# One pool of nine weight tiles, loaded in the order of use, in a fused attention and gated feed-forward kernel

## The chip, the cores and the metric

The kernel runs on one core of a Trainium2 chip. The metric is the time of one execution in microseconds (us), and the median of several runs where there are several. The profiled execution comes with its own time and with its span, from the first to the last instruction that the profile records.

## What is computed

For 2048 tokens of width 1024 (bf16), after a layer norm without scale and bias:

```python
xn = layernorm(x)
q, k, v = split(xn @ wqkv)                  # 32 heads of 32
# each token looks at itself and 7 earlier tokens, 2 apart
logits = einsum(q, k[pos - 2*w]) * 32**-0.5 # w = 0..7, masked below position 0
o = softmax(logits) weighted sum of v[pos - 2*w]
s = o @ wo
g = silu((silu(xn @ w1) * (xn @ w3)) @ w2)  # 3584 hidden columns
out = x + s * g
```

Here w1 and w3 are 1024 x 3584, w2 is 3584 x 1024, wqkv is 1024 x 3072, wo is 1024 x 1024.

## The kernel before

**Tiling.** The tokens are worked on in four blocks of 512 (`c` = 0 to 3). All matrix products are on TensorE (PE), as matmuls of a 128x128 weight tile by 512 columns, accumulated over the contraction. For each block the order on PE is: the qkv projection (`qkv`, line 289; 192 matmuls), the up projections by w1 and w3 (`up_block`, line 270; 14 column blocks `fb` of 32 matmuls each), the first half of the down projection by w2 (`down_half` with `dh` = 0, line 463; 7 tiles of 16 matmuls), the second half (`dh` = 1, again 7 tiles), with the output projection by wo (`wo_proj`, line 432; 64 matmuls) put into it. In block 0 three up blocks come ahead of the qkv projection (`LEAD`), and wqkv is first loaded raw, reordered on VectorE (DVE) and ScalarE (ACT), used from the reordered tiles `pm`, and written to a scratch tensor `wperm`, from which later blocks load it. In block 3 `wo_proj` stands between the two halves, and the second half is `last_half` (line 498), token tile by token tile.

**The attention.** Logits, softmax and the weighted sum run on DVE and ACT beside the matmuls. They are cut into small items in `Side`, which deals them out between the matmuls by costs written by hand. Two shuffles across partitions go through DMAs that GpSimd (POOL) issues: `L` from `E` (line 349) and `Pr` from `pb` (line 390). The weighted sum `oT` (lines 401 and 412) has to be complete before `wo_proj` of the block.

**The weights.** No weight but wo and the raw wqkv is held: each block streams the others again, in tiles of 512 KB (4 KB on each of 128 partitions). All of these loads are issued on the queue of SyncE (SP), which issues in the order of the program and stands still while the instruction at its head waits. A load waits for the last matmul that read the tile whose place it takes. There are two pools:

- `wstream`, six tiles: w1, w3 and the q tiles (from `wperm`). `load_w()` (line 167) issues the next of `w_list`, `take_w` hands out the oldest. At the end of the list stand four w2 tiles for `last_half`.
- `w2s`, three tiles: w2. `load_w2()` (line 185) and `take_w2` do the same with `w2_list`.

An up block loads two further tiles when its own two are used up, but not in its last three column blocks (`AHEAD` = 3). A qkv tile loads one. In the down projection each used w2 tile loads the w2 tile three further on, and `late_w` loads q tiles for the next block (in block 3: the four w2 tiles) at positions written out by hand: in block 0 at tiles 6, 7, 8, 9, 11 and 12 of 14, in blocks 1 and 2 at 1, 3, 5, 7, 9 and 11. Three w2 tiles are loaded before the loop over the blocks, ahead of their use by the whole up projection.

**What shares the SP queue.** Also on SP: the input tiles `x_t` of the next block (line 214), their transposes into `xnT_next` (line 238), `wo` (line 196, eight DMAs of 256 KB), the residual `xres` (line 488, 1 MB), and the writes to `wperm` (line 686). In block 0, `wo` is loaded after down tiles 0 and 2 and `xres` after tile 4; in the other blocks `wo` after up blocks 11 and 12 and `xres` after up block 13. Every load of every queue runs on the same 16 DMA engines of the core.

Of the kernel before, what the change touches and what calls it, by code (L numbers as in the profile page):

```python
# [9 lines left out]
BF16 = mybir.dt.bfloat16  # L10
# [35 lines left out]
def kernel(  # L46
# [11 lines left out]
    nc = tc.nc  # L58
    P = 128
# [4 lines left out]
    NCH = S // CH  # L64
    NST = CH // P
    FT = F // P
    FB = FT // 2
# [4 lines left out]
    LEAD = 3  # L72
    WO_AT = 3
    WO_AT0 = 6
    AHEAD = 3
    PV_GATE = (13.0, 20.0, 20.0, 18.0)
    scale = float(Dh) ** -0.5

# [4 lines left out]
    w2_r = B_w2.rearrange("(ft p) n -> p ft n", p=P)  # L83
# [7 lines left out]
    xp = ctx.enter_context(tc.tile_pool(name="x", bufs=NST))  # L91
    small = ctx.enter_context(tc.tile_pool(name="small", bufs=4))
    xnT_pool = ctx.enter_context(tc.tile_pool(name="xnT", bufs=2))
    wstream = ctx.enter_context(tc.tile_pool(name="wstream", bufs=6))
    w2s = ctx.enter_context(tc.tile_pool(name="w2s", bufs=3))
    qkv_pool = ctx.enter_context(tc.tile_pool(name="qkv", bufs=1))
    hp = ctx.enter_context(tc.tile_pool(name="hT", bufs=FT))
    sgp = ctx.enter_context(tc.tile_pool(name="sg", bufs=3))
# [13 lines left out]
    for st in range(2):  # L112
# [12 lines left out]
        out=ident[:], in_=ident[:], compare_op=ALU.not_equal, fill=1.0,  # L125
# [5 lines left out]
        out=maskb[:], in_=maskb[:], compare_op=ALU.is_ge, fill=-1.0e9,  # L131
# [7 lines left out]


    w_list = []
    for fb in range(LEAD):
        w_list += [("1", fb), ("3", fb)]
    for fb in range(LEAD, FB):
        w_list += [("1", fb), ("3", fb)]
    for c in range(1, NCH):
        w_list += [("q", b) for b in range(12)]
        for fb in range(FB):
            w_list += [("1", fb), ("3", fb)]
    w_list += [("2", fb) for fb in range(4)]  # L150
    w_next = iter(w_list)
    w_tiles = deque()

    def load_w():
        item = next(w_next, None)
        if item is None:
            return
        kind, i = item
        wt = wstream.tile([P, KT, 2 * P], BF16, tag="w")
        if kind == "q":  # L160
            src, dst = wperm[:, :, 2 * i:2 * i + 2, :].rearrange("kt kp tj p -> kp kt (tj p)"), wt[:]
        elif kind == "2":
            src = w2_r[:, i * 4:(i + 1) * 4, 512:1024]
            dst = wt[:].rearrange("p a b -> p (a b)").rearrange("p (i n) -> p i n", n=512)
        else:
            src, dst = (w1_r if kind == "1" else w3_r)[:, :, i * 256:(i + 1) * 256], wt[:]
        nc.sync.dma_start(out=dst, in_=src)  # L167
        w_tiles.append((item, wt if kind != "2" else dst))

    def take_w(item):  # L170
        got, wt = w_tiles.popleft()
        assert got == item, (got, item)
        return wt

    w2_list = [(c, dh, fb) for c in range(NCH) for dh in range(2) for fb in range(7) if (c, dh) != (NCH - 1, 1) or fb >= 4]
    w2_next = iter(w2_list)
    w2_tiles = deque()

    def load_w2():
        item = next(w2_next, None)  # L180
        if item is None:
            return
        c, dh, fb = item
        wt = w2s.tile([P, 4, 512], BF16, tag="w2")
        nc.sync.dma_start(out=wt[:], in_=w2_r[:, fb * 4:(fb + 1) * 4, dh * 512:(dh + 1) * 512])
        w2_tiles.append((item, wt))

    def take_w2(item):
        got, wt = w2_tiles.popleft()
        assert got == item, (got, item)  # L190
        return wt

# [58 lines left out]
    def bring_one():  # L251
        if brings and brings[0][0] <= side.now:
            brings.popleft()[1]()

    def gate_up(g_ps, u_ps):
        sg = sgp.tile([P, CH], BF16, tag="sg")
        nc.scalar.activation(out=sg[:], in_=g_ps[:], func=ACTF.Silu)  # L257
        ht = hp.tile([P, CH], BF16, tag="ht")
        nc.vector.tensor_mul(ht[:], sg[:], u_ps[:])  # L259
        return ht  # L260

    def up_block(c, xnT, fb):
        hts = []
        w1t, w3t = take_w(("1", fb)), take_w(("3", fb))
        for i in range(2):
            pss = []
            for wt in (w1t, w3t):
                ps = psum_mm.tile([P, CH], FP32, tag="mm", name=f"gu{c}_{fb}_{len(pss)}")
                for kt in range(KT):
                    nc.tensor.matmul(  # L270
                        ps[:], lhsT=wt[:, kt, i * P:(i + 1) * P], rhs=xnT[:, kt, :],
                        start=(kt == 0), stop=(kt == KT - 1),
                    )
                pss.append(ps)
            if i == 1 and fb < FB - AHEAD:
                load_w()
                load_w()
            hts.append(gate_up(*pss))
            if c == 0 or c == NCH - 1 or fb < FB - 1:
                side.step(2 * GRP, 0.7)  # L280
            else:
                side.now += 2 * GRP
            bring_one()
        return hts
# [156 lines left out]
    def silu_acc(acc, w=512):  # L441
        gt = ep.tile([P, 512], FP32, tag="gt", bufs=5)
        nc.scalar.activation(out=gt[:, 0:w], in_=acc, func=ACTF.Silu)  # L443
        return gt

    def finish(c, st, c0, w, gt, s_sb, xres, queue):
        g0 = (c * NST + st) * P
        o_t = ep.tile([P, 512], BF16, tag="o_t")
        nc.vector.tensor_mul(gt[:, 0:w], gt[:, 0:w], s_sb[:, st, c0:c0 + w])  # L449
        nc.vector.tensor_add(o_t[:, 0:w], gt[:, 0:w], xres[:, st, c0:c0 + w])  # L450
        queue.dma_start(out=out_flat[g0:g0 + P, c0:c0 + w], in_=o_t[:, 0:w])  # L451

    def down_half(c, dh, hts, at=None):
        accs = [psum_mm.tile([P, 512], FP32, tag="mm", name=f"acc{c}_{dh}_{st}") for st in range(NST)]
        gts = []
        for fb in range(7):
            w2t = take_w2((c, dh, fb))
            order = [(i, st) for i in range(4) for st in range(NST)]
            if fb in (0, 6):
                order = [(i, st) for st in range(NST) for i in range(4)]  # L460
            for n, (i, st) in enumerate(order):
                f = fb * 4 + i
                nc.tensor.matmul(  # L463
                    accs[st][:], lhsT=hts[f][:, st * P:(st + 1) * P], rhs=w2t[:, i, :],
                    start=(f == 0), stop=(f == FT - 1),
                )
                if n == 7:
                    side.step(GRP)
            load_w2()
            late_w(c, dh, fb)  # L470
            if fb == 6:
                gts = [silu_acc(accs[st][:]) for st in range(NST)]
            side.step(GRP)
            if at is not None:
                at(fb)
        return gts

    def late_w(c, dh, fb):
        at = dh * 7 + fb
        if c + 1 < NCH:  # L480
            if at in ((6, 7, 8, 9, 11, 12) if c == 0 else (1, 3, 5, 7, 9, 11)):
                load_w()
        elif at in (1, 3, 5, 6):
            load_w()

    def load_xres(c):
        xres = block("xres").rearrange("p (st d) -> p st d", st=NST)
# [2 lines left out]

    def last_half(c, hts, s_sb, xres):
        dh = 1
        w2ts = [take_w(("2", fb)) for fb in range(4)] + [take_w2((c, dh, fb)) for fb in range(4, 7)]
        for st in range(NST):
            for c0, cut in ((0, 384), (384, 128)) if st == NST - 1 else ((0, 512),):
                acc = psum_mm.tile([P, 512], FP32, tag="mm", name=f"acc{c}_{dh}_{st}_{c0}")
                for f in range(FT):
                    nc.tensor.matmul(  # L498
                        acc[:, 0:cut], lhsT=hts[f][:, st * P:(st + 1) * P],
                        rhs=w2ts[f // 4][:, f % 4, c0:c0 + cut],  # L500
                        start=(f == 0), stop=(f == FT - 1),
                    )
                gt = silu_acc(acc[:, 0:cut], cut)
                finish(c, st, dh * 512 + c0, cut, gt, s_sb, xres, nc.sync)
# [71 lines left out]
    def part0(k, st):  # L576
# [24 lines left out]
        out=junk[:], in_=x0[2][:], func=ACTF.Square, bias=nm[:], scale=1.0 / 32.0, accum_out=mv0[2][:, 1:2],  # L601
# [74 lines left out]
    for t in range(3):  # L676
# [8 lines left out]
        for half in range(2):  # L685
            nc.sync.dma_start(
                out=wperm[half * 4:(half + 1) * 4, :, t * NJ:(t + 1) * NJ, :].rearrange("kt kp j p -> kp kt (j p)"),
                in_=pmh[t, half].rearrange("kp kt j p -> kp kt (j p)"),
            )
    for _ in range(3):  # L690
        load_w2()


    for c in range(NCH):
# [3 lines left out]
        for fb in range(LEAD if c == 0 else 0, FB):  # L698
            blk_hts = up_block(c, xnT, fb)
            hts = hts + blk_hts if hts is not None else blk_hts  # L700
            if c > 0 and fb in (11, 12):
                was.append(load_wo(fb - 11))
            if c > 0 and fb == 13:
                res["x"] = load_xres(c)
        while brings:
            brings.popleft()[1]()
        def early(fb, c=c, res=res, was=was):
            if c == 0 and fb == 4:
                res["x"] = load_xres(c)
            if c == 0 and fb in (0, 2):  # L710
                was.append(load_wo(fb // 2))

        gts = down_half(c, 0, hts, early)
        xres = res["x"]
        if c + 1 < NCH:
# [51 lines left out]
```

## Time and profile before

| | |
|---|---|
| time, median of 3 runs | 818.49 us (818.47 to 820.02) |
| profiled execution: time / span | 818.31 us / 816.5 us |
| mean granted clock of TensorE | 0.999 of full |
| DVE / ACT / POOL busy | 481.7 us (59%) / 205.8 us (25%) / 92.3 us (11%) |
| moved by DMA | 152.69 MB, mean 187 GB/s |
| weight tiles from w1, w3, w2 | 168 loads of 512 KB, median 4.5 us from issue to landing |
| q tiles from `wperm` | 36 loads of 512 KB, median 4.5 us |

Lines such as L463 are lines of the kernel. "A <- B" after an operation names what it writes and reads; in a list of waits it names who waited for whom. The chain of waits is followed back from the last instruction: each piece is the work that the next piece had to wait for, so the pieces add up to the span. In tables by stretch of time, "DMA share" is the mean busy share of the 16 DMA engines; it can read slightly above 1.

### The profile page before, as it was taken

The numbers are of one execution on the slowest core, as the hardware profiler recorded it, in microseconds if no ns is written. First come the engines' busy times: TensorE is split into PE (matmuls) and PEld (weight loads), VectorE is DVE, ScalarE is ACT, GpSimd is POOL, SyncE is SP. The second block draws the span as 40 slices with busy tenths as digits, with TensorE's granted clock in tenths as the row PEclk, the third lists the DMA queues.
The fourth block names the chain that finished last, engine by engine and source line by source line (L and its number), as shares of the span: only waits on it lengthen the run. The fifth ranks groups of instructions, "written<-read, shape, count | busy, mean of one in ns | idle before, by whom it ended". The sixth has DMA issues, their size and how long they took to land.

```text
span 816.5 us, 9661 instructions
## 1 busy us (share of the span) xinstructions
PE 809.4 (99%) x3881; PEld 372.5 (46%) x3881; DVE 481.7 (59%) x489; ACT 205.8 (25%) x319; POOL 92.3 (11%) x172
## 2 busy tenths in 40 slices
PE   9999999999999999999999999999999999999998
PEld 6444444444444444444444444444444444444444
DVE  6629957792229866692224967469311595639622
ACT  5552123011332132101233213310223311311120
POOL 0000032200100223100110021300001004040010
PEclk9999999999999999999999999999999999999999
DMA  9992696797355799947265589995736547696620
GB/s 290 348 375 83 194 210 144 176 287 232 120 150 149 215 203 213 239 142 228 98 199 150 148 213 217 209 210 180 213 118 180 151 138 195 166 217 144 218 92 27
DMA packets 222109, 152.69 MB, mean 187 GB/s; under 512 B 19696, under 2 KB 209136, under 8 KB 222064
## 3 DMA queue, kind: packets, MB, share of 16 engines
q1 hardware_dynamic: 216336, 139.74, 62.6%
q0 software_dynamic: 5440, 12.07, 6.5%
q8 instruction: 30, 0.49, 0.3%
q10 hardware_dynamic: 288, 0.26, 0.1%
q14 instruction: 15, 0.12, 0.1%
HBM read 130.02 MB, written 10.49 MB: 172 GB/s over the span
## 4 chain that ended last, share of the span: by engine, by line
PE 97%; DMA 2%; SPq 0%; DVE 0%; issue 0%; ACT 0%
PE gu L270 45%; PE ps_qkv L289 20%; PE acc L463 20%; PE ps_wo L432 7%; PE acc L498 3%; DMA wt<-in_B_w_dram 2%; PE gu L289 2%; PE gu L579 1%; PE tp L561 0%; SPq L113 0%; SPq L167 0%; SPq L115 0%; DVE gt L449 0%; DVE o_t L450 0%; ACT gt L443 0%
## 5 line engine op out<-in xcount | busy, mean ns | idle before, releaser
L270 PE MATMUL gu<-xnT_next,wt 128*128 128x512 bf16 x1344 | 290.6, 379 | 0.0
L270 PEld LDWEIGHTS <-wt 128*128 128x128 bf16 x1696 | 165.9, 98 | 200.1
L463 PE MATMUL acc<-wt,ht 128*128 128x512 bf16 x784 | 170.5, 379 | 1.8 <-DMA wt<-in_B_w_dram 1.8
L259 DVE TENSOR_TENSOR ht<-sg,gu 128x512 bf16<-128x512 bf16 x112 | 75.8, 683 | 96.9 <-PE gu L270 74.4
L257 ACT ACTIVATE sg<-gu 128x512 bf16<-128x512 f32 x112 | 65.7, 598 | 244.2 <-PE gu L270 243.2
L289 PE MATMUL ps_qkv<-xnT_next,wt 128*128 128x512 bf16 x576 | 124.8, 379 | 0.0
L319 DVE TENSOR_TENSOR prod<-qT,kT 128x4096 bf16<-128x4096 bf16 x32 | 73.1, 2286 | 86.2 <-ACT kT L293 86.1
L463 PEld LDWEIGHTS <-ht 128*128 128x128 bf16 x784 | 76.7, 98 | 94.5 <-issue 2.1
L289 PEld LDWEIGHTS <-wt 128*128 128x128 bf16 x640 | 62.6, 98 | 75.3
L449 DVE TENSOR_TENSOR gt<-gt,s_sb 128x512 f32<-128x512 f32 (+2 forms) x33 | 22.2, 674 | 117.7 <-ACT gt L443 63.6
L270 PE MATMUL gu<-xnT,wt 128*128 128x512 bf16 x352 | 76.1, 379 | 0.0
L349 POOL DMA_DIRECT2D L<-E x64 | 37.1, 587 | 298.6 <-DVE E L334 191.2
L401 DVE TENSOR_TENSOR pv<-Pr,vT 128x4096 bf16<-128x4096 bf16 x28 | 63.3, 2287 | 0.0
L330 DVE TENSOR_TENSOR prod<-prod 128x2048 bf16<-128x2048 bf16 x64 | 61.2, 956 | 1.4
L432 PE MATMUL ps_wo<-wo,oT 128*128 128x512 bf16 x256 | 55.9, 379 | 0.0
L443 ACT ACTIVATE gt<-acc 128x512 f32<-128x512 f32 (+2 forms) x33 | 19.3, 584 | 141.4 <-PE acc L463 120.0
L390 POOL DMA_DIRECT2D Pr<-pb x64 | 36.8, 583 | 106.3 <-DVE pb L383 79.8
L451 POOL DMA_DIRECT2D out_dram<-o_t x28 | 15.3, 547 | 287.2 <-DVE o_t L450 283.6
L289 PE MATMUL ps_qkv<-xnT,pm 128*128 128x512 bf16 x192 | 41.6, 379 | 0.0
L432 PEld LDWEIGHTS <-oT 128*128 128x128 bf16 x256 | 25.1, 98 | 30.2
L436 ACT CAST s_sb<-ps_wo 128x512 bf16<-128x512 f32 x32 | 18.7, 585 | 77.9 <-PE ps_wo L432 77.9
L412 DVE TENSOR_TENSOR oT<-oT,pv 128x4096 bf16<-128x4096 bf16 x16 | 36.6, 2290 | 0.3
(66 smaller groups left out, 370.2 us busy)
## 6 DMA issues: line engine op xcount, KB each, us to landing
wt<-in_B_w_dram SPq DMA_DIRECT2D x168, 512.0 KB, 4.5
wt<-wperm SPq DMA_DIRECT2D x36, 512.0 KB, 4.5
wo<-in_A_wo_dram SPq DMA_DIRECT2D x32, 256.0 KB, 9.1
raw<-in_A_wqkv_dram SPq DMA_DIRECT2D x6, 1024.0 KB, 10.1
wperm<-pm SPq DMA_DIRECT2D x6, 1024.0 KB, 9.6
L<-E POOLq DMA_DIRECT2D x64, 64.0 KB, 6.3
Pr<-pb POOLq DMA_DIRECT2D x64, 64.0 KB, 4.4
xres<-in_A_x_dram SPq DMA_DIRECT2D x4, 1024.0 KB, 10.7
```

What stands on the lines that cost most here:

```text
L257: nc.scalar.activation(out=sg[:], in_=g_ps[:], func=ACTF.Silu)
L259: nc.vector.tensor_mul(ht[:], sg[:], u_ps[:])
L270: nc.tensor.matmul(ps[:], lhsT=wt[:, kt, i * P:(i + 1) * P], rhs=xnT[:, kt, :], start=(kt == 0), stop=(kt == KT - 1),)
L289: nc.tensor.matmul(ps[:], lhsT=lhs(kt), rhs=xnT[:, kt, :], start=(kt == 0), stop=(kt == KT - 1))
L319: nc.vector.tensor_mul(prod, qT[:], kT[:, :, o:o + CH])
L330: nc.vector.tensor_add(prod[:, 0:n, :], prod[:, 0:n, :], prod[:, n:2 * n, :])
L349: nc.gpsimd.dma_start(out=L4[sq * 32:(sq + 1) * 32, r, :, :], in_=E[r * 32:(r + 1) * 32, :, sq * P:(sq + 1) * P],)
L390: nc.gpsimd.dma_start(out=Pr[r * 32:(r + 1) * 32, :, sq * P:(sq + 1) * P], in_=pb[sq * 32:(sq + 1) * 32, :, :],)
L401: nc.vector.tensor_mul(dst, Pr[:, w, :].unsqueeze(1).to_broadcast([P, NJ, CH]), vT[:, :, o:o + CH])
L412: nc.vector.tensor_add(a, a, b)
L432: nc.tensor.matmul(ps[:], lhsT=oT[:, j, st * P:(st + 1) * P], rhs=was[dh][:, j, :], start=(j == 0), stop=(j == NJ - 1),)
L463: nc.tensor.matmul(accs[st][:], lhsT=hts[f][:, st * P:(st + 1) * P], rhs=w2t[:, i, :], start=(f == 0), stop=(f == FT - 1),)
```

## The change

The pool `w2s`, its list and its two functions are gone, and so are `late_w` and `AHEAD`. `wstream` has nine tiles, which takes the same memory as six and three did. `w_list` holds all 204 weight tiles in the order in which they are taken: for each block (the q tiles, except in block 0), w1 and w3 by turns, and 14 w2 tiles. Before the loop over the blocks 15 tiles have been issued and six taken; from there on each tile that is taken is followed, once used, by one load. So an up block loads two tiles in all of its 14 column blocks, and a qkv or a down tile loads one.

```diff
-    AHEAD = 3
...
-    wstream = ctx.enter_context(tc.tile_pool(name="wstream", bufs=6))
-    w2s = ctx.enter_context(tc.tile_pool(name="w2s", bufs=3))
+    wstream = ctx.enter_context(tc.tile_pool(name="wstream", bufs=9))
...
+    for c in range(NCH):
+        if c > 0:
+            w_list += [("q", b) for b in range(12)]
         for fb in range(FB):
             w_list += [("1", fb), ("3", fb)]
-    w_list += [("2", fb) for fb in range(4)]
+        w_list += [("2", dh * 7 + fb) for dh in range(2) for fb in range(7)]
...
         elif kind == "2":
-            src = w2_r[:, i * 4:(i + 1) * 4, 512:1024]
+            dh, fb = divmod(i, 7)
+            src = w2_r[:, fb * 4:(fb + 1) * 4, dh * 512:(dh + 1) * 512]
...
-            if i == 1 and fb < FB - AHEAD:
+            if i == 1:
                 load_w()
                 load_w()
...
-            w2t = take_w2((c, dh, fb))
+            w2t = take_w(("2", dh * 7 + fb))
...
-            load_w2()
-            late_w(c, dh, fb)
+            load_w()
...
-        w2ts = [take_w(("2", fb)) for fb in range(4)] + [take_w2((c, dh, fb)) for fb in range(4, 7)]
+        w2ts = [take_w(("2", 7 + fb)) for fb in range(7)]
...
     for _ in range(3):
-        load_w2()
+        load_w()
```

The matmuls, their order, and the items of `Side` with their places are the same in both kernels.

More of the change, by code (lines that the diff above doesn't have):

```diff
@@ L141 @@
     w_list = []
[L142 to L147, printed above, removed]
+    for c in range(NCH):
+        if c > 0:
+            w_list += [("q", b) for b in range(12)]
         for fb in range(FB):
             w_list += [("1", fb), ("3", fb)]
-    w_list += [("2", fb) for fb in range(4)]
+        w_list += [("2", dh * 7 + fb) for dh in range(2) for fb in range(7)]
     w_next = iter(w_list)
@@ L171, in take_w @@
         got, wt = w_tiles.popleft()
[L172 to L189, printed above, removed]
         assert got == item, (got, item)
@@ L476, in down_half @@
         return gts
[L478 to L484, printed above, removed]
     def load_xres(c):
```

## The prediction

> **What bounds the kernel now.** I read the busy times first, then the chain of waits, then the list of all waits of PE, then the stretch in which the one relevant wait falls.
>
> From the page (busy us, share of the span; then the chain by engine):
>
> ```profile
> PE 809.4 (99%) x3881; PEld 372.5 (46%) x3881; DVE 481.7 (59%) x489; ACT 205.8 (25%) x319; POOL 92.3 (11%) x172
> ...
> PE 97%; DMA 2%; SPq 0%; DVE 0%; issue 0%; ACT 0%
> ```
>
> PE is busy nearly throughout. A change of loads adds and removes no matmul, so it can gain only where PE stands still, and lose only where it makes PE stand still anew. The waits of PE (total us, times, longest):
>
> ```profile
> PE acc L463 <- DMA wt<-in_B_w_dram: 1.8, 1, 1.8
> PE warm_ps L539 <- DVE warm L119: 1.2, 1, 1.2
> PE gu L579 <- ACT xnT L565: 0.5, 1, 0.5
> ```
>
> Two of the three are in the first 10 us and have nothing to do with this pool. One wait for a weight tile is left, in the whole span. The chain between 147 and 175 us (start, us, what) shows where:
>
> ```profile
> 146.91 1.08 PE gu L270 x5
> 147.99 13.83 PE acc L463 x64
> 161.82 0.02 issue
> 161.84 8.66 DMA wt<-in_B_w_dram
> 170.50 0.04 issue
> 170.54 4.48 PE acc L463 x20
> ```
>
> It is in block 0, first half of the down projection. 64 matmuls take 13.83 us, so one takes 0.216 and a tile of 16 takes 3.45. The tile that was late is the seventh (fb = 6): w2s has three places, so it was issued at 161.84, when the fourth tile was used up. PE had two tiles left, 6.9 us, and wanted it at 147.99 + 96 x 0.2158 = 168.71. It took 8.66 us, and PE went on at 170.54: 1.83 us lost. SP's queue shows why it was slow (start, us, line, count):
>
> ```profile
> 158.82 1.98 SPq L196 DMA_DIRECT2D wo<-in_A_wo_dram  x4
> 161.84 3.84 SPq L185 DMA_DIRECT2D wt<-in_B_w_dram  x2
> 165.73 0.50 SPq L488 DMA_DIRECT2D xres<-in_A_x_dram  x1
> ```
>
> 1 MB of wo was issued just ahead of it, another tile and 1 MB of xres behind. The table by stretch (columns: PE, PEld, DVE, ACT, POOL busy, clock, DMA share, GB/s) confirms it, and shows what stands empty shortly before:
>
> ```profile
> 134.00:141.00 7.00, 7.00 (x34) 3.21 (x33) 5.07 (x5) 1.19 (x2) 2.77 (x5) 1.00 0.14 28
> 141.00:148.00 7.00, 7.00 (x34) 3.13 (x33) 1.38 (x2) 1.19 (x2) 6.42 (x12) 1.00 0.56 113
> ...
> 158.50:162.00 3.50, 3.50 (x18) 1.57 (x17) 3.46 (x2) 0.00 (x0) 0.00 (x0) 1.00 1.10 309
> 162.00:165.50 3.50, 3.50 (x18) 1.57 (x16) 3.47 (x3) 0.00 (x0) 0.00 (x0) 1.00 1.14 239
> ```
>
> The DMA engines are full during the wait, and were nearly idle from 134 to 141, when the last up blocks loaded nothing.
>
> **The change, part by part.**
>
> *Lead of the loads.* With nine places a load is issued when the tile nine earlier is used up, so eight tiles lie between: 8 x 3.45 = 27.6 us in the qkv and down phases. In the up phase two tiles are used together and the worse of a pair has three blocks of 6.9, 20.7 us. Before it was 6.9 (w2), 13.8 (up) and 17.3 (q). The longest landing of a weight tile in the whole trace is 12.7 us (in the first 60 us), 10.6 in the up phase of block 0. 20.7 exceeds every one of them, so no tile should be late: **-1.83 us** in block 0. The other blocks have no wait to remove, since PE's list holds just the one: 0.
>
> *Up blocks 11 to 13 now load.* In block 0 the pairs are issued at the block ends, 134.2, 141.1 and 148.0, so w2 tiles 0 to 8 are all under way when the down projection begins, in stretches at share 0.14 and 0.56. Seventh tile: issued 148, wanted 168.7. The traffic at 152 to 173 is as dense as before (one tile per 3.45 us, 2 MB of wo, 1 MB of xres), but its tiles are wanted from 179 on.
>
> *SP.* The added loads wait for PE, and behind them on SP in blocks 1 to 3 are wo (after blocks 11 and 12) and xres (after 13). Before, wo went out at 330.0 in block 1; now at the ends of up blocks 11 and 12, 336.5 and 343.4, and xres at 350.3. They land in 9 to 11 us (median 9.1 and 10.7), by 361; wo is wanted at 384.81 and xres at 387.9: over 20 us of cover. In block 3: 737, 744 and 751, landed by 762, wanted at 775.04. 0. The transposes into xnT_next start their last at 131, 313 and 513 us, before up block 11 ends in its block: not touched.
>
> *late_w removed, q tiles in turn.* Same 204 loads, same bytes; q tile 0 goes out at about 169 in place of 174.6, its `wperm` was issued by 53.8 and lands in at most 12.7, by 66.5. 0.
>
> *The start.* Loads 7 and 8 no longer wait for the first pair's places. But SP reached them only at 18.77, behind the raw loads, with the DMA engines full (share 1.13 from 10 to 20 us, 1.09 from 40 to 50), and the order of issue is unchanged. I take 0. The only weight wait there is 0.9 us at the weight loads of L579, before 10 us; if something freed it, -0.9 is the lower end. Upper end 0: nothing is issued ahead of what it stood behind.
>
> *Pr beside the new loads in block 0.* Its 16 DMAs run 138.2 to 147.4, median 2.0 us each on idle DMA engines; now 3 MB of w2 tiles run beside them. Blocks 2 and 3 show 6.0 and 6.1 beside traffic, and from their first Pr issue to the first oT it is 18.0 and 17.5 us, against 10.8 in block 0: oT may be up to 7.2 later. It ends now at 183.04, wo_proj would begin at 194.88 - 1.83 = 193.05. 10.0 of cover, 2.8 left in the worst case. 0 on the path.
>
> *The rest.* oT of blocks 1 to 3 ends at 371.8, 574.7 and 769.0, wo_proj begins at 384.8, 585.1 and 775.0; both ends follow PE and move together. The last seven w2 tiles are issued by 768, before 775.5 as it was, and wanted at 787. 0.
>
> **Sum.** Against the profiled execution: span 816.5 - 1.83 = 814.67, and 1.81 around it, gives 816.48. The median of the runs is 818.49, 0.18 above the profiled one, and would give 816.66. I forecast 816.6, the middle: 0.22 to 0.23% less.
>
> [...] The row: one gap of 1.83 us, in one of four blocks. [...] I hold that a single gap with its releaser named is enough for its own length, and no more than that.
>
> The row: 8.66 us for 512 KB, median 4.5. [...]
>
> **Rivals.**
> 1. *The wait moves, no gain.* The DMA engines are over 1.0 from 155 to 172 us; if the backlog, not the lead, is what counts, another tile of block 0 is late by as much. Against: the nine tiles ahead hold 31 us of work and the backlog would have to grow by 20.7. Also in this case: the change doesn't get its depth (a load waits for a place later than I counted). Price: 0 to 1.83 given back, 816.7 to 818.5.
> 2. *Slower, through Pr and oT in block 0.* The new w2 loads slow the Pr shuffle, oT is late, and `wo_proj` stands on PE waiting for it. It begins to cost when oT is over 10.0 us later; the rows of blocks 2 and 3 give 7.2. To end over 0.2% slower (1.64 us) the delay must reach 10.0 + 1.83 + 1.64 = 13.5, nearly twice those rows: 820.1 and more there.
> 3. *More than the gap.* The 0.9 us at the start goes too: 815.7.
>
> **How the numbers follow.** A measurement of this kernel can tell about 0.2% (1.64 us, below 816.85) from no change, and the forecast gain is just 0.19 above that. Chances: gap closed 0.82, rival 1 0.11, rival 2 0.05, rival 3 0.02. Of the first I give 0.70 to a result below 816.85 and 0.12 to one between it and 817.2 by scatter. Faster 0.70 + 0.02 = 0.72; same 0.12 + 0.10 = 0.22; slower 0.05 + 0.01 = 0.06. Range: low 815.7 (rival 3's bound), high 818.5 (rival 1's whole price).
>
> **What would show it.** Right: the wait of PE at L463 for wt gone, the chain one piece of PE from 9.3 us to 813 - 1.8, DMA share at 134 to 148 us up to near 1, `wo_proj` of block 0 at 193.0, oT before it. Wrong: any new wait of PE for wt, oT or xnT; a landing over 20 us; wo of blocks 1 to 3 landing after PE wants it; a first matmul at a different time than 7.6 us.

## The result, and the profile after

| | before | after |
|---|---|---|
| median of 7 runs | 818.49 us (818.09 to 820.02) | 816.18 us (816.0 to 816.7) |
| profiled execution: time / span | 818.31 / 816.5 us | 816.18 / 814.4 us |
| after / before | | 0.997, 95% interval 0.9959 to 0.9982 |

The medians differ by 2.31 us, 0.28%. The interval, 0.18 to 0.41% less, excludes equal times, but its near end falls just short of the 0.2% that the prediction takes as what a measurement of this kernel can tell. The forecast was 816.6. Three profiled executions of kernels further down took 1067 to 2230 us; they are left out of all medians, and traces of these kernels come from single runs made later. (Lines of the changed kernel have other numbers: the down projection is L441 in place of L463, the loads are all L163.)

All waits of PE in the profile after; the wait for a w2 tile is gone, and what is left belongs to the first 10 us:

```profile
PE warm_ps L508 <- DVE warm L117: 1.2, 1, 1.2
PE gu L548 <- ACT rs L519: 0.7, 1, 0.7
PE gu L548 <- DMA wt<-in_B_w_dram: 0.2, 1, 0.2
```

The weight loads of PE (PEld) date its progress better than the matmuls here, since none of the 3881 is missing from the trace after, where 74 matmul records are. From 160 to 175 us (start, us, what, count), first before:

```profile
159.92 8.52 PEld L463 LDWEIGHTS <-ht 128*128 128x128 bf16 x40
170.55 4.41 PEld L463 LDWEIGHTS <-ht 128*128 128x128 bf16 x21 [2.11 <-issue]
```

and after:

```profile
160.01 14.99 PEld L441 LDWEIGHTS <-ht 128*128 128x128 bf16 x70
```

Before, the loads stop for 2.11 us, of which 0.12 is their ordinary spacing (0.216 per matmul less 0.098 of load): 1.99 lost. After, 70 follow each other without a break. That is nearly the whole difference of the spans: the first weight load of the down projection of block 0 comes at 147.62 before and 147.50 after (0.12), the first of wo_proj at 194.50 and 192.39 (2.11 = 0.12 + 1.99), and the spans end 2.1 apart. Nothing else on PE moved.

The late tile is still slow. SP's queue after, around its issue:

```profile
158.70 1.98 SPq L174 DMA_DIRECT2D wo<-in_A_wo_dram  x4
161.72 3.84 SPq L163 DMA_DIRECT2D wt<-in_B_w_dram  x2
165.65 0.46 SPq L457 DMA_DIRECT2D xres<-in_A_x_dram  x1
```

The same issue at the same time between the same neighbours, and the landing of that one tile in the trace after:

```profile
wt<-in_B_w_dram SPq DMA_DIRECT2D x1, 512.0 KB, 8.6
```

8.6 us, where it was 8.7. But it is now w2 tile 12, which PE wants eight tiles later. The DMA engines by stretch:

```profile
134.00:141.00 7.00, 6.95 (x33) 3.14 (x32) 4.94 (x5) 1.19 (x2) 2.89 (x6) 1.00 0.62 180
141.00:148.00 7.00, 6.95 (x33) 3.21 (x33) 1.40 (x3) 1.19 (x2) 6.33 (x11) 1.00 0.96 257
158.50:162.00 3.50, 3.50 (x18) 1.61 (x17) 3.50 (x2) 0.00 (x0) 0.00 (x0) 1.00 1.10 315
162.00:165.50 3.50, 3.50 (x18) 1.61 (x17) 3.43 (x3) 0.00 (x0) 0.00 (x0) 1.00 1.13 228
```

The stretch ahead of the down projection has filled (share 0.14 to 0.62, 0.56 to 0.96); the crowded one is as crowded as it was (1.10 and 1.13, where it was 1.10 and 1.14).

### The profile page after: what moved, and what is told of

Same layout as the page of the kernel before. It is cut to its first block, busy times and chain, and to the rows that moved or that the text cites. A ratio compares the mean times of both kernels' runs of the same rounds, so it can differ in the third digit from the quotient of the medians.

```text
span 814.4 us, 9639 instructions
## 1 busy us (share of the span) xinstructions
PE 804.9 (99%) x3807; PEld 372.4 (46%) x3881; DVE 481.7 (59%) x489; ACT 205.6 (25%) x319; POOL 92.6 (11%) x172
## 4 chain that ended last, share of the span: by engine, by line
PE 95%; DVE 2%; issue 1%; DMA 1%; ACT 1%; SPq 0%; DVEq 0%
PE gu L248 42%; PE acc L441 21%; PE ps_qkv L267 20%; PE ps_wo L410 7%; PE acc L467 3%; PE gu L267 2%; DMA wt<-in_B_w_dram 1%; PE gu L548 1%; DVE stats L179 1%; DVE ht L237 0%; ACT L235 0%; DVE mx L358 0%; DVE x_t L182 0%; DVE z L356 0%; ACT sg L235 0%
## 5 line engine op out<-in xcount | busy, mean ns | idle before, releaser
L441 PE MATMUL acc<-wt,ht 128*128 128x512 bf16 x768 | 169.3, 379 | 0.8
L441 PEld LDWEIGHTS <-ht 128*128 128x128 bf16 x784 | 76.7, 98 | 92.5
```

Of the source, the lines that this page charges most:

```text
L441: nc.tensor.matmul(accs[st][:], lhsT=hts[f][:, st * P:(st + 1) * P], rhs=w2t[:, i, :], start=(f == 0), stop=(f == FT - 1),)
```

## The experiments

Two theories were held against each other. *Lead against landing*: a tile is late by its landing time less the time between its issue and its use, and only that counts. *Something else in the change*: the one pool, the order of use, the loading in a nearly idle stretch, or the start.

### Nine tiles again

The changed kernel as it is.

> The changed kernel as it is, beside the following three on the same chip. Theory (lead): the one gap of PE, 1.99 us by the starts of the weight loads (168.44 + 0.12 to 170.55), is closed and nothing else changes; the time is 816.2 to 816.6, 1.9 to 2.3 us below the kernel before, and PE has no wait for wt in the down projection. Rival (start): the first weight load of the down projection in block 0 lay 0.12 us earlier in the changed kernel (147.50 against 147.62), and some of the gain beyond 1.99 is the start's; if that is the change's doing, it is 147.5 again; if it is scatter, it moves by 0.1 to 0.3 between runs of the same kernel.

Measured: 816.43 us, ratio to before 0.997 (0.9958 to 0.9981). And its profile from a later single run:

> A second undisturbed profile of the changed kernel, for the scatter of the start: the first weight load of the down projection of block 0 was at 147.50 here, 147.62 in the kernel before and 147.41 and 147.44 in two others. Expected between 147.3 and 147.8, with no wait for wt at L441, the granted clock 1.0 from 10 us on, and a time of 816.0 to 816.8.

816.07 us; no wait for wt on PE; the first weight load of the down projection at 147.38. In the other profiles of this page it lies between 147.41 and 147.88, and at 148.41 in one, for kernels of either kind; so the 0.12 of the start is scatter and no part of the change.

### wo and xres of block 0 earlier, both old pools kept

```diff
-            if c > 0 and fb in (11, 12):
+            if fb in (11, 12):
                 was.append(load_wo(fb - 11))
-            if c > 0 and fb == 13:
+            if fb == 13:
                 res["x"] = load_xres(c)
...
-            if c == 0 and fb == 4:
-                res["x"] = load_xres(c)
-            if c == 0 and fb in (0, 2):
-                was.append(load_wo(fb // 2))
```

> The kernel before, with both its pools, but in block 0 wo goes out after up blocks 11 and 12 and xres after 13, as in the other blocks, so that no large load stands between the w2 tiles. Theory (lead against landing): the seventh tile was late since it took 8.7 us against a lead of 6.9; without 3 MB beside it it takes 3.5 to 5 us, as in the other blocks, so the gap goes and the time is 816.2 to 816.7, with the pools untouched. Rival (depth): three places for w2 are too few and a deeper pool is what was needed; then the gap stays, 818.3 to 818.6. On the path to wo_proj: Pr runs beside 2 MB of wo and may take 2 to 7 us longer, oT ends at 185 to 190, before 192.4.

Measured: 816.45 us, ratio 0.997 (0.9958 to 0.9981). SP's queue:

```profile
132.29 4.77 SPq L196 DMA_DIRECT2D wo<-in_A_wo_dram  x8
137.14 0.42 SPq L488 DMA_DIRECT2D xres<-in_A_x_dram  x1
151.31 17.64 SPq L185 DMA_DIRECT2D wt<-in_B_w_dram  x6
```

The tile issued at 161.6 lands in 3.8 us, against a lead of 6.9 that is unchanged, and PE doesn't wait. So the deeper pool was not needed for this gain: taking 3 MB out of the way gives the same. The price was paid off the path: Pr took 6.4 us in place of 2.0 (medians) and oT ended at 187.1, still 5.2 ahead of wo_proj (192.34).

### Nine tiles, no loads in the last three up blocks

```diff
-            if i == 1:
+            if i == 1 and fb < FB - 3:
                 load_w()
                 load_w()
...
                 if i == 1:
                     load_w()
+                    if b < 6:
+                        load_w()
...
             load_w()
+            if c == NCH - 1 and fb in (1, 3, 5, 6):
+                load_w()
```

> One pool of nine in the order of use, but its depth is not used in the down projection: up blocks 11 to 13 load nothing (as before the change), so three w2 tiles are held when the down projection begins and the lead is two tiles, 6.9 us; six extra loads in the first six q tiles of the next block fill the pool again, four in block 3. Theory (lead): the gap in block 0 is back at the seventh tile, 1.8 to 2.0 us, and the time is 818.0 to 818.7, as before the change. Rival (order and pool): the single list in the order of use, or one pool in place of two, or the start, made the gain; then the time stays at 816.2 to 816.6 and no wait of PE for wt shows.

Measured: 816.7 us, ratio 0.9971 (0.996 to 0.9983): the gap did not come back, as the rival had it. The trace of a single run tells why:

> A profile of the pool of nine without loads in the last three up blocks. If SP runs ahead since the places are free, the w2 tiles 3 to 8 and the first half of wo of block 0 are issued before 148 us, between 127 and 140, with no wait for PE between them, and no tile is late. Rival: they are issued one per down tile from 151 on and land in under 6.9 us for another reason.

816.35 us, and on SP:

```profile
132.56 0.37 SPq L163 DMA_DIRECT2D wt<-in_B_w_dram  x1
132.99 2.71 SPq L174 DMA_DIRECT2D wo<-in_A_wo_dram  x4
135.79 4.06 SPq L163 DMA_DIRECT2D wt<-in_B_w_dram  x2
139.90 2.20 SPq L174 DMA_DIRECT2D wo<-in_A_wo_dram  x4
142.20 4.56 SPq L163 DMA_DIRECT2D wt<-in_B_w_dram  x2
```

The loads that stand after down tiles 0 to 4 in the program go out from 132 to 147, before PE has begun the first of these tiles at 147.7. They waited for places, not for positions, and six places came free as the last three up blocks used up their tiles. The edit moved loads in the text but did not shorten the lead, and wo went ahead with them. So it did not test the theory, and the next one was made.

### Nine tiles, six q tiles ahead of w2 tile 3

```diff
     for c in range(NCH):
         if c > 0:
-            w_list += [("q", b) for b in range(12)]
+            w_list += [("q", b) for b in range(6 if c == 1 else 0, 12)]
...
-        w_list += [("2", dh * 7 + fb) for dh in range(2) for fb in range(7)]
+        for at in range(14):
+            if c == 0 and at == 3:
+                w_list += [("q", b) for b in range(6)]
+            w_list += [("2", at)]
```

(`take_w` looks its tile up in the list.)

> The lead-two run did not do what it was meant to: with free places in the pool SP needs no used-up tile and runs ahead of PE, so leaving loads out of the up blocks gave no short lead. Here the pool of nine and every call of the load stay as changed, and only the order of the list differs in block 0: after w2 tiles 0 to 2 come q tiles 0 to 5, then w2 tiles 3 to 13. The six q tiles hold six places through the down projection, so w2 has three and a lead of two tiles, 6.9 us, with wo and xres where they were. Theory (lead): the gap of about 2 us is back at the seventh w2 tile of block 0, and the time is 818.0 to 818.8, as before the change. Rival (one pool, or loading while the DMA engines are idle, whatever is loaded): the six q tiles use the idle stretch just as well; 816.2 to 816.8.

Measured: 820.13 us, ratio 1.001 (0.9997 to 1.0023): all of the gain is gone, in the same pool, with the same loads.

> A profile of the pool of nine with six q tiles ahead of w2 tile 3 in block 0. Theory (lead): PE waits for wt at the seventh w2 tile of block 0, issued at about 161.7 and landing in 8 to 9.5 us, 1.8 to 2.5 us by the gap of its weight loads; where the gap is near 2.1 (as in the kernel before) the granted clock stays at 1.0 after it, where it is near 2.5 (as in the run of the cut alone) it drops to about half for some 3.4 us and costs 1.7 us more. Rival (pool or idle stretch): no wait for wt.

819.6 us, span 817.8. SP's queue in that trace:

```profile
132.75 15.90 SPq L166 DMA_DIRECT2D wt<-wperm  x6
151.74 0.37 SPq L166 DMA_DIRECT2D wt<-in_B_w_dram  x1
```

And PE's weight loads:

```profile
147.88 13.91 PEld L445 LDWEIGHTS <-ht 128*128 128x128 bf16 x65
163.35 6.79 PEld L445 LDWEIGHTS <-ht 128*128 128x128 bf16 x32 [1.56 <-issue]
171.85 4.20 PEld L445 LDWEIGHTS <-ht 128*128 128x128 bf16 x20 [1.72 <-issue]
```

The quiet stretch was used all the same, by q tiles that PE wants from 213 on. The w2 tiles had a lead of two, and two of them were late: the fifth (issued 155.2, 8.1 us to land) and the seventh (162.1, 9.7 us). 1.56 + 1.72 - 2 x 0.12 = 3.04 us lost; I had expected only the seventh. The clock stayed at 1.0. What the places hold, in the order of use, is what counts.

### Seven tiles

```diff
-    wstream = ctx.enter_context(tc.tile_pool(name="wstream", bufs=9))
+    wstream = ctx.enter_context(tc.tile_pool(name="wstream", bufs=7))
...
-    for _ in range(3):
+    for _ in range(1):
         load_w()
```

> The changed kernel with seven places in place of nine (one load in place of three before the loop over the blocks), 8 KB per partition less. Theory (lead): the lead is six tiles, 20.7 us, in the down phases and at least two blocks, 13.8 us, in the up phases; the longest landing of a weight tile after the first 60 us was 8.7, so no tile is late and the time is that of nine, 816.2 to 816.6. Rival (backlog): the DMA engines are full from 155 to 173 us and the nine tiles held are what bridges it; then some of the gap is back, 0.5 to 2 us, at L441 in block 0.

Measured: 816.66 us, ratio 0.997 (0.9959 to 0.9982), no wait for a w2 tile; the longest landing of a weight tile between 72 and 790 us was 9.5. Nine are not needed. `last_half` takes seven at once, so fewer were not tried.

### Two places for w2

```diff
-    w2s = ctx.enter_context(tc.tile_pool(name="w2s", bufs=3))
+    w2s = ctx.enter_context(tc.tile_pool(name="w2s", bufs=2))
...
-    w_list += [("2", fb) for fb in range(4)]
+    w_list += [("2", fb) for fb in range(5)]
...
```

(The places where the tiles are loaded and taken follow.)

> The kernel before with two places for w2 in place of three (the fifth of the last seven tiles goes to the other pool), so a lead of one tile, 3.45 us. Theory (lead against landing): each of the w2 tiles costs its landing less 3.45 us. In the down phases of blocks 1 to 3 the median landing of a w2 tile is 3.4 to 3.6 us, up to 5.4, so 0.1 to 0.4 us for most of some 14 tiles a block, 4 to 12 us in all; in block 0, where landings from 3.6 to 8.7 us were seen, 8 to 16 us more; 830 to 848 us. Rival (throughput): the DMA engines are only 0.56 busy in those phases, so two places do as well there, and block 0 loses a few us at most; 819 to 824.

Measured: 835.99 us, ratio 1.0202 (1.0181 to 1.0222). The profiled run was 837.05, its span 835.3. Its wait line for w2:

```profile
PE acc L463 <- DMA wt<-in_B_w_dram: 12.7, 17, 2.9
```

By the weight loads there are 28 gaps in the four down projections, from 0.17 to 3.17 us, 17.6 in all less their ordinary spacing: 6.6, 3.6, 6.2 and 1.2 by block. Against a kernel without a gap (814.4) the span is 20.9 longer, so 3.3 are missing. The table by stretch after the two longest gaps (2.93 and 3.17 us; the granted clock is the last number but two) has them:

```profile
163.00:168.00 5.00, 5.00 (x18) 1.98 (x17) 5.00 (x3) 0.00 (x0) 0.00 (x0) 0.69 0.94 181
595.00:600.00 5.00, 4.49 (x14) 1.70 (x14) 0.00 (x0) 0.00 (x0) 0.00 (x0) 0.66 0.15 49
```

The granted clock fell to 0.69 and 0.66 on the mean of 5 us, some 1.6 us each, 3.3 together. The theory holds in the other direction too, with that as a surcharge on long gaps; DMA share was 0.44 to 0.61 in the down phases of blocks 1 to 3, so throughput was not short there.

### Four places for w2, and the cut that pays for them

```diff
-    w2s = ctx.enter_context(tc.tile_pool(name="w2s", bufs=3))
+    w2s = ctx.enter_context(tc.tile_pool(name="w2s", bufs=4))
...
-    sgp = ctx.enter_context(tc.tile_pool(name="sg", bufs=3))
+    sgp = ctx.enter_context(tc.tile_pool(name="sg", bufs=2))
...
-        gt = ep.tile([P, 512], FP32, tag="gt", bufs=5)
+        gt = ep.tile([P, 512], FP32, tag="gt", bufs=4)
...
-        o_t = ep.tile([P, 512], BF16, tag="o_t")
+        o_t = ep.tile([P, 512], BF16, tag="o_t", bufs=1)
...
-    for _ in range(3):
+    for _ in range(4):
         load_w2()
```

> The kernel before with four places for w2, a lead of three tiles, 10.4 us; the memory comes from other pools (four gt tiles for five, two sg for three, one o_t for two), and the next kernel has that cut alone. Theory (lead): 10.4 exceeds the 8.7 us of the late tile, the gap is gone, and the time is 1.9 to 2.3 us below that of the cut alone; where the cut costs nothing, 816.2 to 816.8. Rival (backlog): wo and xres hold the DMA engines full and the next tile is late in its turn; a gap of 0.5 to 2 us stays.

> The kernel before with four gt tiles, two sg tiles and one o_t tile, and w2 with its three places. Both theories: the gap stays, 1.8 to 2.0 us. The cut itself: ACT and DVE stand idle 243 us and more waiting for PE, so I expect no cost, 818.3 to 819.0; should a wait for a gt, sg or o_t place appear on PE, it is in the run with four places too and falls out of the difference.

Measured: 818.0 us with four (0.9985, 0.9975 to 0.9994), 819.94 with the cut alone (1.0012, 1.0 to 1.0024): 1.94 us between them, and no wait for w2 in the trace with four. A lead of three tiles is enough. That the cut is free was wrong: the chain with four ends with 1.62 us in which the last o_t waits for the only o_t place (1.63 in the cut alone). It falls out of the difference.

The profiled run of the cut alone was 822.54, span 820.7, and shows a gap a little longer than the kernel before has:

```profile
162.54 6.79 PEld L463 LDWEIGHTS <-ht 128*128 128x128 bf16 x32 [0.22 <-issue]
171.87 0.31 PEld L463 LDWEIGHTS <-ht 128*128 128x128 bf16 x2 [2.54 <-issue]
172.44 0.15 PEld L463 LDWEIGHTS <-ht 128*128 128x128 bf16 x1 [0.27 <-issue]
...
175.00 0.15 PEld L463 LDWEIGHTS <-ht 128*128 128x128 bf16 x1 [0.28 <-issue]
175.43 1.46 PEld L463 LDWEIGHTS <-ht 128*128 128x128 bf16 x7 [0.27 <-issue]
```

The table by stretch just before and after 172.1 (PE's busy time is the number behind the comma, the granted clock the last but two):

```profile
168.72:172.13 3.41, 1.15 (x7) 0.43 (x5) 3.38 (x2) 0.00 (x0) 0.00 (x0) 1.00 1.08 356
172.13:175.54 3.41, 3.41 (x10) 1.22 (x9) 3.38 (x3) 0.89 (x2) 0.00 (x0) 0.50 1.01 352
```

From 172.0 to 175.4 the weight loads are 0.43 us apart in place of 0.216, and the clock reads 0.50 for 3.41 us: 2.54 us of standing still cost another 1.7.

The length of the gap need not be what decides. In the clock record the clock was full for 167.25 us before this fall and at 0.50 for 3.41 us behind it, and in the first profile of the kernel before it was full for 808.96 us: 49, 1 and 237 times 3.413 us. A step, in what follows, is that length, counted on from the first entry of the record. Each of the three falls behind a gap, here and with two places, lasted one step. In the step before it PE was busy for 1.15 us here and for 0.76 and 0.68 us with two places. The gap of the kernel before, 2.11 us, lies across two steps (the 48th and 49th of its record, which begins at 6.28 us):

```profile
166.71:170.12 3.41, 2.00 (x10) 0.78 (x8) 3.38 (x3) 0.00 (x0) 0.00 (x0) 1.00 1.07 326
170.12:173.53 3.41, 2.98 (x14) 1.36 (x14) 3.38 (x2) 1.39 (x3) 0.00 (x0) 1.00 1.06 376
```

So the place of a gap against the steps goes with the fall as well as its length does. No trace here has a gap of 2.1 us within one step, and which of the two counts stays open.

### The kernel before again

> A second profile of the kernel before, for the size of the gap. Its 29 runs on this day's chips range from 818.0 to 821.9, with granted clocks of 0.997 to 0.998 in those above 820. If the gap and what it does to the clock make that spread, the gap by the weight loads lies between 2.0 and 2.7 us, with the clock at 1.0 after it where the run is near 818.3, and at about half for some 3 us where the run is above 820. Rival: the spread comes from the start of the kernel, and the gap is 2.1 in every run.

818.61 us; its weight loads:

```profile
162.01 6.79 PEld L463 LDWEIGHTS <-ht 128*128 128x128 bf16 x32 [0.36 <-issue]
170.86 4.20 PEld L463 LDWEIGHTS <-ht 128*128 128x128 bf16 x20 [2.07 <-issue]
```

A gap of 2.07 after one of 0.36 (the tile before was late by 0.24 as well), and the clock at 1.0 behind it, as in the first profile (2.11). So two runs near 818.4 had a short gap and no loss of clock. Nine of 29 runs of this kernel beside the experiments with q tiles ahead, two places, four places and the cut alone took over 820 us, and all nine have mean granted clocks of 0.997 to 0.998; the other 20 have 0.999 or 1.0. Half speed for 3.4 of 817 us is a mean of 0.998. It fits that in those runs the clock fell behind the gap, because the gap was longer or because it lay within one step; none of them was profiled, so this stays inferred.

## Why the prediction was right, by its steps

- **Bound and place.** PE bounds the kernel (busy for 99% of the span, 97% of the chain before), and its one wait in block 0 was what the change could gain. Shown: the gap is gone and the rest of the program is as long as it was. Of the signs named beforehand one cannot be read: the chain after is not one piece but 246, 95% of it PE, in a trace that lacks 74 matmul records.
- **Size of the gap.** 1.83 forecast, 1.99 measured by the weight loads. The term was taken from the matmuls, whose records last 0.379 us though one starts every 0.216; a gap counted from the end of a record is short by the difference, 0.16.
- **2.31 by the medians.** 1.99, and scatter. The kernel before scatters upwards (818.0 to 821.9 in those 29 runs) and the changed one does not (816.0 to 816.91 in 13 timed runs). A surcharge in clock behind the gap, as in the cut alone (0.50 for 3.41 us), is the likely reason, not a shown one; the prediction priced a wait at its length and did not have it.
- **Lead.** 8 tiles in the down phases, three blocks in the up phases: no tile late, and seven places do as well. Four places for w2, or no wo beside it, close the gap as well, and q tiles in the places of w2 reopen it. The lead of the tiles next in use, held against their landing, is the cause. One date in the prediction is wrong: the seventh w2 tile went out at 141.0, and 148 (147.9 in the trace) is the ninth's. So its cover was 7 us larger than stated.
- **The nearly idle stretch before the down projection** was read rightly, but it is not the cause: "Nine tiles, six q tiles ahead" fills it and has the gap. Nor did the positions of the loads in the up blocks matter where places were free (816.7 us without loads in the last three).
- **SP.** wo of block 1 was expected at 336.5 and 343.4 and went out at 334.8 and 341.7, xres at 348.9 for 350.3 (PE being 2 us ahead by then), landing in 7 to 9 us. No effect, as forecast.
- **Pr and oT in block 0 (rival 2).** Pr's median rose from 2.0 to 3.9 us beside the w2 tiles, oT began 1.9 us later (150.95 for 149.06; up to 7.2 allowed) and ended at 184.9, 7.5 before wo_proj. Even with wo and xres there too it was 5.2. Rival 2 was far off.
- **Rival 1 (backlog)** fell: seven places suffice, and so do four for w2.
- **Rival 3, the 0.9 us at the start**, did not come: the start scatters by some tenths, once by 0.8 us, with no part of the change in it.
- **One gap, one slow tile.** One gap in four blocks was worth 1.99 us and came from too few places for the traffic beside it: the late tile took 8.7 us behind wo, and tiles took 3.4 to 3.9 with wo moved.

## What to carry to other kernels

Where the bounding engine waits once for a streamed tile, compare that tile's landing with its lead (places less one, by the use of one tile), and look at what was issued just ahead of it: here more places for the tiles next in use (816.2 us) and moving the big neighbour (816.45 us) each closed the gap, and one was enough. A list in the order of use over one pool gives every phase the lead of the whole pool, where here the fixed pools left the w2 tiles of block 0 a lead of 6.9 us while the six places of the other pool stood free from 148 us until its next load at 174.6. Price a wait at its length at least, and look whether the clock falls behind it, as it did here behind a gap of 2.54 us (0.50 for 3.41 us) and not behind one of 2.11.

## What the runs showed of the hardware

- A gap of 2.54 us in PE's weight loads was followed by 3.41 us at half rate (clock 0.50); gaps of 2.93 and 3.17 likewise (0.69 and 0.66 over 5 us); gaps of 2.11, 2.07 and 1.72 were not. In the 3.41 us ahead of each of these three falls PE was busy for 0.68 to 1.15 us. The gap of 2.11 lies across two stretches of that length in which PE was busy for 2.00 and 2.98, and no fall came. Whether the length of the gap or its place decides is not shown.
- A w2 tile of 512 KB in the down projection of block 0 took 3.4 to 3.9 us to land with wo and xres moved away. Among them on the same queue it took 3.5 to 9.7, and 6.5 to 9.7 where it stood right behind 1 MB of wo.
- A DMA went out when its place was free and SP had reached it: as six places came free, the load written behind the first down tile was issued at 132.56, 15 us before PE began that tile at 147.69.
